# Due times of a list scheduler, nudged job by job from a table (linear attention and a token/channel mixer on one core)

## The chip, the core and the metric

The kernel runs on one core of one Trainium2 chip. The metric is the device time of one execution in microseconds (us); the runs shown are repeated executions of the same program. All times below are in microseconds unless marked ns.

## The reference

Inputs are q, k and v of 8 batches x 8 heads x 1024 positions x 64, two projections E and F (64 x 1024), and four mixer weights. Shortened:

```python
k_proj = einsum('ks,bhsd->bhkd', E, k)
v_proj = einsum('ks,bhsd->bhkd', F, v)
scores = q @ k_proj.T / sqrt(64)
attn   = softmax(scores)                       # over 64 projected positions
x      = attn @ v_proj                         # heads side by side: 8 x 1024 x 512
h      = maximum(x.T @ w_tok1, 0) @ w_tok2     # 1024 -> 256 -> 1024, over the positions
u      = x + h.T
out    = u + maximum(u @ w_ch1, 0) @ w_ch2     # 512 -> 1536 -> 512, over the channels
```

## The kernel before, in words

Each of the 8 batches goes through a front and a back. The front loads q, k and v (`load_heads`, L354, in halves of four heads from batch 1 on, on the POOL queue), projects k and v over the positions (`kv_proj`, matmuls at L492 and L495), brings kT and qT into place, computes scores (`scores`, L605, exponentials on ACT at L614), attends (`attend` or `attend_whole`, L628 and L664, division on DVE at L640, L645, L676 and L681), and runs the token mixer (`token1...`, `token2...`) to get u. From batch 2 on, kT and qT come from DMA transposes on SP's queue (L524 and L570), and u is turned to uT the same way in two halves (`turn_u`, L767). The back handles each batch in two blocks of 512 positions (16 blocks, counted by j): DVE forms sums S of quarters of uT (`s_sums`, L789), `up_set` forms seven products in place of eight for each of three slices of the channels (matmuls at L1152; ACT and DVE bring the results into G at L1174, L1180 and L1133, and DVE forms sums of G at L1188), and `down_block` multiplies G by the second weight, again with seven products (L1261), empties the banks on DVE (L1301, L1311) and stores (L1295, on the POOL queue; the last block's stores go on SP and ACT). Sums of the channel weights that the seven-product form needs are made on DVE at the start (`combine`, L452).

The order of all this is not written by hand. Every step is a `Job` with an engine, an estimated occupation and latency, dependencies, a claim on PSUM banks where it has one, and a due time `prio`. Due times are set by formulas: the back by `due_u` and `due_d` (24.65 units for each block), the front spread evenly between a beginning and an end by `front`, and steps without a due time get one from the steps that follow them. `Planner.plan` is a list scheduler: it walks through time, takes for each engine the jobs that can start within 0.02 of the earliest, and among these picks the one with the lowest due time. Its result is sorted by planned start and issued in that order. Each engine then works in that order, with semaphores for the dependencies; so the due times decide the order of the instructions on each engine, and nothing else. Three details matter below:

- Loads and stores to POOL's queue are marked `early`: they are put into the order at the time at which their dependencies end, not at which the planner lets them move. Loads that become free together keep the order in which the planner picked them.
- Loads and transposes take turns by added dependencies (`tie`). The first v half of a later batch has to have landed before the second half of u is turned; the second v half and q are issued after that transpose has landed; the two qT transposes wait for the last q load.
- The idle time of PE in the plan at the start is filled with matmuls on zeros (L413), as long as bank 5 is unused.

Before the scheduling loop, the due times of all jobs later than -30 get a pseudo-random offset of at most 0.8 either way, from the job's number and a seed.

Of the kernel before, what the change touches and what calls it, by code (L numbers as in the profile page):

```python
# [11 lines left out]
ALU = mybir.AluOpType  # L12
ACT = mybir.ActivationFunctionType
EARLY = 12.0
SHAKEN_FROM = -30.0
SHAKE = 1.6
SEED = 710
WHOLE = 3
TWO = 2
SUMS = 60.0  # L20
# [27 lines left out]
class Planner:  # L48
# [37 lines left out]
    def plan(self):  # L86
# [13 lines left out]
                j.prio = max((d.prio for d in j.deps), default=0) + 2  # L100


        for j in self.jobs:
            if j.prio > SHAKEN_FROM:
                j.prio += SHAKE * ((j.n * j.n * 7919 + j.n * SEED * 31 + SEED * SEED * 17) % 10007 / 10007 - 0.5)
        free = {}
        waiting = {j.n: len(j.deps) for j in self.jobs}
        can = {}
# [19 lines left out]
        def home(b, now):  # L128

            if held[b.stream] + b.span > self.caps[b.stream]:  # L130
                return None
            if b.span == 2:
                free2 = [
                    (max(now, bank_free[i], bank_free[i + 1]), i) for i in PAIRS[b.stream]
                    if bank_free[i] is not None and bank_free[i + 1] is not None
                ]
                return (*min(free2)[:1], 0, 0, min(free2)[1]) if free2 else None
            if b.stream in "UD" and turn[b.stream][0] is not b:
                return None
            best = None  # L140
            keep = [i for i in self.homes["U"] if clean[i] and bank_free[i] is not None]
            if all(clean[:5]):
                keep = []
            for i in self.homes[b.stream]:
                t = bank_free[i]
                if t is None or (b.seeded and not clean[i]):
                    continue
                if not b.seeded and clean[i] and keep and keep[-1] == keep[0] == i:
                    continue
                c = (max(now, t), clean[i], t, i)  # L150
                if best is None or c < best:
                    best = c
            return best

        while any(can.values()):
            pick = None
            for e, js in can.items():
                f = free.get(e, 0.0)
                cands = []
                for j in js:  # L160
                    t = max(f, est[j.n])
                    spot = None
                    if j.takes:
                        h = home(j.takes[0], t)
                        if h is None:
                            continue
                        t, spot = h[0], h[3]
# [4 lines left out]
                c = min((c for c in cands if c[0] <= t0), key=lambda c: (c[1], c[2]))  # L172
# [4 lines left out]
            t, _, _, j, spot = pick  # L177
# [4 lines left out]
            if j.takes:  # L182
                b = j.takes[0]
# [1351 lines left out]
```

## Time and profile before

| | us |
|---|---|
| median of 3 runs | 422.15 |
| lowest and highest run | 421.42, 422.19 |
| span of the profiled execution, first to last instruction | 420.3 |
| what lies around the span, against the median | 1.85 |
| PE busy | 410.3 |
| DVE busy | 347.5 |
| ACT busy | 231.3 |
| POOL busy | 66.2 |

The profile is of one execution, whose own time is given by its span alone; the granted TensorE clock was 1.000 over it. The five engines named are PE (matmuls; PEld is the loading of its weights), DVE, ACT, POOL and SP, which issues transposes and the last stores. A DMA's landing is told as the time from the start of its issue instruction. "Start to start" below is the distance of the starts of two matmuls that follow each other.

### The profile page before, as it was taken

The page shows a single profiled execution, that of the slowest core. Times are in us where ns is not written, and L with a number is a line of the kernel's source. Part 1 is how long each engine was busy: PE and PEld are TensorE (multiplying, and loading weights), DVE is VectorE, ACT ScalarE, POOL GpSimd, SP SyncE. Part 2 cuts the span into 40 slices and gives each one's busy share as a digit, 9 for nine tenths or more (in the row PEclk, how much of TensorE's full clock was granted, in tenths as well). Part 3 has the DMA queues.
Part 4 walks back from the last instruction along what each step waited for, and adds up shares of the span by engine and source line. Part 5 has one row for each costly group of instructions (what it writes and reads, how often), then busy time and mean ns, then how long its engine had stood idle before and what let it go on. Part 6 is the DMA issues. An engine that isn't in the chain of part 4 may idle for free.

```text
span 420.3 us, 9411 instructions
## 1 busy us (share of the span) xinstructions
PE 410.3 (98%) x3824; PEld 347.6 (83%) x3838; DVE 347.5 (83%) x747; ACT 231.3 (55%) x444; POOL 66.2 (16%) x104
## 2 busy tenths in 40 slices
PE   7899999999999999999999999999999999999996
PEld 4587877688788888888988898888798899988885
DVE  2359969679779798998979799797979999978685
ACT  2958885356646555555547455475655554454430
POOL 8443220022003030032002110112100000010010
PEclk9999999999999999999999999999999999999999
DMA  9999999989994989398998897395962501251223
GB/s 166 207 201 206 207 206 166 238 137 204 174 152 88 194 138 251 60 165 159 198 205 130 175 183 194 84 189 100 209 149 50 152 35 67 50 97 56 101 89 114
DMA packets 96668, 62.48 MB, mean 149 GB/s; under 512 B 62064, under 2 KB 92272, under 8 KB 96624
## 3 DMA queue, kind: packets, MB, share of 16 engines
q0 software_dynamic: 34944, 45.09, 54.9%
q1 hardware_dynamic: 61056, 16.00, 22.6%
q10 hardware_dynamic: 624, 0.79, 0.7%
q8 instruction: 30, 0.49, 0.4%
q14 instruction: 14, 0.11, 0.1%
HBM read 59.24 MB, written 16.78 MB: 181 GB/s over the span
## 4 chain that ended last, share of the span: by engine, by line
PE 87%; DMA 6%; DVE 4%; issue 1%; POOL 1%; ACT 0%; POOLq 0%; DVEq 0%
PE psum L1261 34%; PE psum L1152 33%; PE psum L856 4%; PE psum L972 4%; DMA v_sb<-in_v_dram 3%; DMA q_sb<-in_q_dram 3%; PE psum L492 3%; PE psum L605 3%; PE psum L664 2%; DVE u L1079 1%; PE psum L628 1%; PE psum L695 1%; PE psum L719 1%; PE psum L744 1%; PE psum L589 1%
## 5 line engine op out<-in xcount | busy, mean ns | idle before, releaser
L1261 PEld LDWEIGHTS <-G 128*128 128x128 bf16 x1344 | 130.4, 98 | 18.9 <-issue 0.6
L1261 PE MATMUL psum<-wc_sb,G 128*128 128x256 bf16 x768 | 102.9, 273 | 0.3 <-DVE wait L1301 0.3
L1174 ACT ACTIVATE G<-psum 128x512 bf16<-128x512 f32 x96 | 57.3, 599 | 56.8 <-PE psum L1152 56.5
L1152 PEld LDWEIGHTS <-wc_sb 128*128 128x128 bf16 x768 | 74.1, 98 | 10.2
L1261 PE MATMUL psum<-wT,G 128*128 128x256 bf16 x576 | 77.6, 273 | 0.3
L1188 DVE TENSOR_TENSOR G<-G 128x512 bf16<-128x512 bf16 (+1 forms) x140 | 69.6, 519 | 1.0
L1152 PEld LDWEIGHTS <-wT 128*128 128x128 bf16 x576 | 55.7, 98 | 9.0 <-issue 0.8
L1152 PE MATMUL psum<-S,wc_sb 128*128 128x256 bf16 x384 | 57.6, 273 | 0.2
L1152 PE MATMUL psum<-uT,wc_sb 128*128 128x256 bf16 x384 | 57.6, 273 | 0.0
L1152 PE MATMUL psum<-S,wT 128*128 128x256 bf16 x384 | 55.7, 273 | 0.2 <-DVE S L789 0.2
L1295 POOL DMA_DIRECT2D out_dram<-o x30 | 16.4, 546 | 240.3 <-DVE o L1301 160.5
L614 ACT ACTIVATE a<-psum 128x512 bf16<-128x512 f32 x64 | 36.7, 598 | 17.6 <-PE psum L605 16.5
L1301 DVE TENSOR_TENSOR o<-psum,u 128x512 f32<-128x512 f32 x55 | 37.6, 685 | 9.5 <-PE psum L1261 7.2
L1180 ACT COPY ua<-psum 128x512 f32<-128x512 f32 x48 | 28.2, 588 | 25.5 <-PE psum L1152 25.1
L1133 DVE CUSTOM_DVE_ANT_0 G<-psum,ub 128x512 bf16<-128x512 f32 x48 | 33.0, 687 | 9.1 <-PE psum L1152 8.9
L1133 DVE CUSTOM_DVE_ANT_0 G<-psum,ua 128x512 bf16<-128x512 f32 x48 | 33.0, 688 | 8.0 <-ACT ua L1180 7.8
L1195 ACT COPY psum<-psum 128x512 f32<-128x512 f32 x48 | 27.9, 580 | 14.5 <-PE psum L1152 5.3
L1180 ACT COPY ub<-psum 128x512 f32<-128x512 f32 x48 | 28.2, 587 | 9.4 <-PE psum L1152 8.3
L1152 PE MATMUL psum<-uT,wT 128*128 128x256 bf16 x192 | 28.8, 272 | 0.1
L681 DVE TENSOR_TENSOR x_sb<-psum,rdn 128x512 bf16<-128x512 f32 x40 | 27.5, 688 | 0.6
L605 PE MATMUL psum<-qT,kT 128*128 128x512 bf16 x54 | 19.8, 379 | 1.4 <-ACT kT L557 0.6
L354 POOL DMA_DIRECT2D v_sb<-in_v_dram x18 | 13.5, 751 | 45.8 <-DMA uT<-u 25.0
(108 smaller groups left out, 546.3 us busy)
## 6 DMA issues: line engine op xcount, KB each, us to landing
out_dram<-o POOLq DMA_DIRECT2D x30, 512.0 KB, 4.4
k_sb<-in_k_dram POOLq DMA_DIRECT2D x14, 512.0 KB, 9.5
v_sb<-in_v_dram POOLq DMA_DIRECT2D x14, 512.0 KB, 10.5
q_sb<-in_q_dram POOLq DMA_DIRECT2D x14, 512.0 KB, 9.4
wc_sb<-in_moe_w_ch_dram POOLq DMA_DIRECT2D x6, 256.0 KB, 12.4
wc_sb<-in_moe_w_ch_dram POOLq DMA_DIRECT2D x4, 384.0 KB, 12.2
k_sb<-in_k_dram POOLq DMA_DIRECT2D x4, 256.0 KB, 6.6
v_sb<-in_v_dram POOLq DMA_DIRECT2D x4, 256.0 KB, 7.2
```

The costliest lines, as they stand in the source:

```text
L605: lambda: nc.tensor.matmul(bank(bk), kT[:, h].rearrange("p c k -> p (c k)"), qT[:, h].rearrange("p j s -> p (j s)"), start=True, stop=True,),
L614: lambda: nc.scalar.activation(out=a_t[h // 2 % 2][:, h % 2], in_=bank(bk), func=ACT.Exp, scale=scale),
L681: lambda: nc.vector.tensor_tensor(out=x_sb[:, :, h * D : (h + 1) * D].rearrange("p (n c) d -> p n c d", n=2), in0=view()[:, :, :, 0:D], in ...
L856: nc.tensor.matmul(to, tok1_of(n, si), mv, start=(n == 1 and si == 0), stop=(si == NJ - 1), skip_group_check=True,)
L1133: nc.vector._custom_dve(TENSOR_ADD_SAT, out=out, in0=in0, in1=in1, s0=FMAX, s1=0.0)
L1152: nc.tensor.matmul(t[:, c, :], w1_of(n, dd, 2 * m + c), a_of(j, n, dd), start=(n in (1, 7) and c == 0 and dd == 0), stop=(c == 1 and dd == 1),
L1174: lambda: nc.scalar.activation(out=G[:, n, cs], in_=view(src), func=ACT.Relu),
L1180: 512, lambda: nc.scalar.copy(out=dst, in_=view("y")), writes=[(name, s % 2)],
L1188: 512 * len(both), lambda: f(out=G[:, n, c], in0=G[:, a, c], in1=G[:, b, c]), ps=False,
L1195: 512, lambda: nc.scalar.copy(out=view("y"), in_=view("x")), takes=[bk["y"]],
L1261: nc.tensor.matmul(to, G[:, G_OF[n], cc, t * P : (t + 1) * P], w2_of(n, cc), start=(n in opens and (t == 0 or alone) and cc == 0), stop=(c ...
L1301: 512, lambda: nc.vector.tensor_add(out=dst, in0=view(src), in1=u_of(sh, dh)),
```

## The change

The pseudo-random offset is replaced by one from a table: a string with one character for each job, in the order in which the jobs were added. A character's code less 80, times 0.25, is added to the due time; the characters in use reach from `$` to `}`, which is -11.0 to +11.25. The first 37 characters, and some others, are `P`, which is zero. The table was found by a local search on the planned program. Jobs, dependencies, durations in the planner, tiles and the functions that issue instructions are the same. The built program has 25 matmuls on zeros for 26; otherwise it has the same instructions in another order on every engine, and PSUM banks may be assigned otherwise.

```diff
-SHAKEN_FROM = -30.0
-SHAKE = 1.6
-SEED = 710
+STEP = 0.25
+MIDDLE = 80
+NUDGES = (
+    "PPPPPPPPPPPPPPPPPPPPPPPPPPPPPPPPPPPPPKa%Q]>f}YHB%VmgYjif?GOVZ}@}BpfO5CUF<`,o,TeHoVjRTChfR4S=;^NwbuhZ"
...
+    "v`}}}}rr}jrUY:]R?P/10("
+)
...
-        for j in self.jobs:
-            if j.prio > SHAKEN_FROM:
-                j.prio += SHAKE * ((j.n * j.n * 7919 + j.n * SEED * 31 + SEED * SEED * 17) % 10007 / 10007 - 0.5)
+        for j, c in zip(self.jobs, NUDGES):
+            j.prio += STEP * (ord(c) - MIDDLE)
```

What moves, as far as the two built orders show it: on POOL, stores and loads swap places from the third batch on, and loads of one group change their order; on SP, the place of kT among the two qT transposes in batches 2 to 5 and 7; on PE and DVE, the steps of the front against those of the back, by up to some ten microseconds of work, and the products of a block among each other. The last eight groups of matmuls of the last block (products 5, 2, 3 and 4) and the ten DVE steps that end the program keep their order.

More of the change, by code (lines that the diff above doesn't have):

```diff
@@ L14 @@
 EARLY = 12.0
-SHAKEN_FROM = -30.0
-SHAKE = 1.6
-SEED = 710
+STEP = 0.25
+MIDDLE = 80
+NUDGES = (
+    "PPPPPPPPPPPPPPPPPPPPPPPPPPPPPPPPPPPPPKa%Q]>f}YHB%VmgYjif?GOVZ}@}BpfO5CUF<`,o,TeHoVjRTChfR4S=;^NwbuhZ"
+    "IUGKS[W3H^98N7<TUMs8=OVUf][QuDVXxO]qwD8aR[XgOKSJTA8:Od6SMN'4DTiG.t0f]E]0bZf)f7gQDi_}Zo@FZE.Jm,V?6bT2"
+    "gZBOoPPPPPP+]EB:L?nhNP<RUS-J.MeIO*7$j5UI_L[8.BmbvePPN8BQqTbM[I)TlG:n2MK1[.)@BIh9G0,XtsmCHhvm,yb]<,d>"
+    "MR$FFC|ynr]AQ7EU5bfywyym`]G*N_*DM@AYcJDavgxmsmq]8aQ.06(*NEM]4AR`LtSn{f9,b$+$-.GUqE;E]Lcp[-@[Ykuz@V;O"
+    "HIRFWm^MO|kHV78-7fkm--Z/-<3F[D`}9<[UNGC:NHZaR3vjVXplnzswqbQMfDRlYI8fY|MT]8.<M:]:TbNUZd2]8O?PQ[kHCGRp"
+    "2P$>q,>G}fHlmmC-P]T3D8';{ROXa}V=}0TK@8=*6:82<n63@$773CS;+T[gOWJW,Ngkf$$$+&($(';Q4EPU0)f]0;2)%VMgH&2_"
+    "hEa`?A$/6$+PTUM04aDfHFr2[>,CCJ?^A&rtUl]WRhDR[m]g]MH{yd`?aQO9,0/-)$6=H`-%<%>F%%F0'R$[;w:h8Rfa0NL$canL"
+    "FC$G$${kb[[7fmlfkQ86NG8(}6_:R),165*576*]Gh2:Ml54Jh*&PZ8-rjeqgW1,$%:(&$'9RJ$RB,6LdBHYiT[dfZ]]]]-Wn=XU"
+    "]z$$:)]VBgdD+n^6_mvc}wwhsm}xw}v]OiZ{e`:;TL>YOa&f4>]mM[<cL]][aoRWDY$?YY}}}XR`FqL&&%60dLaXI+1rljVGI$J="
+    "Sv-5J[sD'8L5YZ{S<lf:2EEjrTE'(2D?<S9<.:/0XSO9A*-7$,1<6$.9+3^`?QFE7.MigwlZA;zaZ]NTQ@2&>FN$Z)*$,V1gU]`5"
+    "hA5Q?ANNkXUcjgWZab(EeU{|jbQLG[J_^g8@kP{ePE|]I6S&0Fiew[|m|vOB?Yo@N9EA`.]:2t.WWLH`kJfg{WQxg[R^SQwWnO}E"
+    "fD93=J?J_Q^UYbEGTQ|g`h]?&JHgb`gSI)9rQUfkSdCADY0c$2yQ2./ZI;M]4K.GBE9*H.31^gaNdodFc,-AY:oYfThnn{adLK;4"
+    "S(4/cpb|DmO2V{RlLMST;O*E4,'_5hA)C:85.FZ]s9ROI2Lib($/,'U'66eF<T*9I;D/($'&'4-Y)=(c]A`X=Zc92.3DD1h-&[nw"
+    "]Wvz{frUrhrfF'9%ibB+$J$$V>JE1aJutZh1me00kDjt}R}>i5KJ}Q^iu]}}mF>;}N}{vw[R{^w:Px4]6&WT]CQ>38(OvN{u+xUS"
+    "USr}Ol:>s}NI[R4P`Ae:@]3WMFQY^g`NfYhyv|}2;;&IciBM_)jhp;VqrF]scw}}}t}[qK>LdC}}}FSU2P'ZAEBF78oLkRLdKL.C"
+    "jDOZkLvyKI1QTGDB2(%>HL^we'YIr<7B7OuKetXgWHsXmvU`VnTUwss>|rB]oC*OV-/OIKr$BDRMJb@}anh9YO*b=g}YMh1h}aD^"
+    ".fG}}pWt},<^^jc:7K=<:z)-4$(($-PNP9MT=*7$Q7_aOm|bk0}f$}OtBMG/}rN]GiHIk=e4qk22WebZ3F-jW@M.Ph&>`OuzE$b]"
+    "}|`i{}I`_9iMhXSj99M><3XQk+$XD>+*h&I2f]n8qL/4*a3]q}IRBI-87]4j_s]N:Pep3A?63<UX40QY1>8,Q:J(o*(9(*&lV7^b"
+    "oRROGqFfozup[X52f}(duwq]|w{lifTfNlAlZH$km$JbmQB1F$S_[0{jT_KXC=6DcrGN:.>SS:QDB$4R*E?OlZsmffFaCc$gZF7t"
+    "XYaTew@`fYNXd$cx]eIqO/@)J0,)3,N'?4O,9),:=ca7-/2ZOJ;G$3-I%S%K%$F[4YD0(A]0I'9xoSc]LOCO:'-4-V-?CXgTgC9K"
+    "B^^rgk3R-$1/$5EAFF^Y$&t-b9?$=.F`]cg|WE8al}h>}^]tsgrv]@EMGBcVZVgT@NhGsX[]dY]rN]gdu|[w}>t]>T[O]]$>*5]P"
+    "GRI1{70dO]`rusrNEdVub$_C2L-::d{jbcGY=+oMJJh5)[LtM<O(tm^P`>WKM1+Al-]N]_I>iJMR_G6C&@ZI`GTXlWP3C2]QSIDi"
+    "v`}}}}rr}jrUY:]R?P/10("
+)
```

## The prediction

> **What bounds it now.** I read the page's busy line first, then the stretches of the span, the waits of PE, the chain that ended last around 31 us, the SP queue around 73 us and single places of the timeline. All times are microseconds.
>
> ```profile
> PE 410.3 (98%) x3824; PEld 347.6 (83%) x3838; DVE 347.5 (83%) x747; ACT 231.3 (55%) x444; POOL 66.2 (16%) x104
> ```
>
> PE is the bound, and this change issues the same matmuls. The second view, busy time by stretch (length, then PE, PEld, DVE, ACT, POOL, clock, DMA share, GB/s), says where PE is not busy:
>
> ```profile
> 0.00:40.00 40.00, 35.18 (x387) 25.27 (x391) 21.58 (x66) 24.94 (x57) 22.96 (x38) 1.00 1.18 194
> 40.00:100.00 60.00, 59.39 (x551) 47.45 (x553) 50.55 (x137) 38.97 (x74) 8.36 (x12) 1.00 1.09 194
> 100.00:120.00 20.00, 19.63 (x169) 15.98 (x168) 15.66 (x33) 11.45 (x23) 2.81 (x4) 1.00 1.06 173
> 120.00:408.00 288.00, 287.63 (x2650) 251.76 (x2656) 252.77 (x501) 155.35 (x291) 31.79 (x50) 1.00 0.67 132
> 408.00:416.60 8.60, 8.48 (x77) 7.11 (x74) 6.52 (x14) 0.57 (x1) 0.26 (x1) 1.00 0.30 113
> ```
>
> Half of the 10.0 idle is the start (4.82, most of it inputs coming in at 166 to 207 GB/s), 3.70 lies behind the last matmul. Between 40 and 416.6 only 0.61+0.37+0.37+0.12 = 1.47 is shown. That understates a wait: a 256-column matmul is drawn 273 ns long, while eight of them in the chain take 0.87, so they follow each other every 0.109, and up to 0.164 of each wait lies under the drawn tail of the matmul before. What an order can win is thus small: a handful of waits of 0.15 to 0.6. The waits of PE name them:
>
> ```profile
> PE psum L1093 <- DVE u L1079: 0.6, 2, 0.4
> PE psum L1261 <- DVE wait L1301: 0.3, 1, 0.3
> PE psum L495 <- DMA v_sb<-in_v_dram: 0.3, 1, 0.3
> ```
>
> **What the new order removes.** Only the instruction order of the two built programs is used, with durations from the trace. One filler matmul on zeros goes (25 for 26); it filled a wait, so it counts nothing.
>
> (a) Start, 30 to 36. The chain runs through DVE, and in it stand the channel-weight sums between the additions that PE waits for:
>
> ```profile
> 31.88 0.33 DVE wc_sb L452
> 33.41 0.33 DVE wT L452
> 34.94 0.33 DVE wT L452
> ```
>
> Between the second addition to u and the first S sum the old DVE order has four such sums, the new one two: 2 x 0.33 = 0.66 off that chain. PE waits 0.44+0.20 at L1093 and 0.17 at the S sum, 0.8 in all. The moved sums still have to be there for the first products from wT, so I take 0.5 (0 to 0.8).
>
> (b) At 88. PE waits 0.34 as drawn, and from start to start 0.5, for the DVE addition that empties the bank of product 3 of a down block:
>
> ```profile
> 88.55 0.81 PE L1261 MATMUL psum<-wc_sb,G 128*128 128x256 bf16 x6 [0.34 <-DVE wait L1301]
> ```
>
> Between product 5 and product 3 of that block PE has two attends and one scores now, 2 x 0.113 + 0.216 = 0.44; in the new order an up product of four matmuls stands there too, 0.88. The added 0.44 covers nearly all: 0.4 (0 to 0.5).
>
> (c) At 109, the v load for batch 3. It was issued at 102.71 behind a store of 101.64, landed 7.29 later, and PE lost 0.5. Its issue waits for the second transpose of u (96.32 to 102.14), which waits for the first v half, second of three loads then (landed 96.26). The new POOL order puts that v half first: issued 87.35, it lands after the 5.43 that the first of the three took, at 92.8; transpose 5.82, issue 0.57 later, load 5.4: 104.6. The new PE order reaches this projection 37 matmuls (4.1) earlier, at 109.3-4.1 = 105.2 before the other terms, which move it by about 0.1. It is just in time: saves 0.5 (0 to 0.5).
>
> (d) End. After the last sums of G PE's weight load waits 0.40, from start to start 0.3:
>
> ```profile
> 409.00 7.32 PEld L1261 LDWEIGHTS <-G 128*128 128x128 bf16 x68 [0.40 <-DVE G L1188]
> ```
>
> Twelve matmuls (1.31) now stand between the last up product 4 and product 7, whose sums need 2.0 (406.97 to 409.00). In the new order 34 matmuls (3.7) stand there. Saves 0.3 (0 to 0.4).
>
> (e) Four small waits (39.9, 60.6, 162.2, 260.0; 0.28, 0.15, 0.16, 0.13 from start to start) may go or be replaced by others: I take half, 0.4 (-0.3 to 0.7).
>
> Sum: 0.5+0.4+0.5+0.3+0.4 = 2.1.
>
> **What it adds.** (f) SP's queue, batch 2. Today it runs, with a scores matmul as first reader (start, time in the queue):
>
> ```profile
> 72.80 4.11 SPq L570 DMA_TRANSPOSE qT<-q_sb  x1
> 77.01 2.27 SPq L524 DMA_TRANSPOSE kT<-kb  x1
> 79.33 2.45 SPq L570 DMA_TRANSPOSE qT<-q_sb  x1
> 84.22 0.38 PE L605 MATMUL psum<-qT,kT 128*128 128x512 bf16 x1
> ```
>
> They land 7.94, 4.50 and 5.77 after issue: at 80.75, 81.52 and 85.10. The first scores need kT and the first qT half (81.52, 2.7 spare); the second half is read from 91.7. The new SP order is second half, first half, kT. Both halves are still held until the last q load lands (72.66; those loads keep their POOL order), so the sequence starts at 72.8 again, and now the first scores need all three. In PE's new queue they stand at the same place (779 matmuls ahead, 780 before), so at 84.2 less (a): 83.7. Bounds: kT issued third, at 79.3, and landed after the shortest kT time of the trace, 3.0, is there at 82.4 and costs nothing; landing when the third does now, 85.1, costs 1.4. The 16 engines are full over 72.8 to 85.1 (DMA share 1.01) and the same bytes move, so I stand near the later end: 1.0 (0 to 1.5). Behind the waiting scores stand all PE work, then ACT's exponentials, then DVE's divisions; nothing is hidden.
>
> [...]
>
> (g) The rest of POOL and SP: stores and loads swap places, and kT goes last in batches 3 and 7 too, to the middle in 4 and 5. The tightest of these is batch 3: its first scores stand at about 120.9 (105.2 plus 15.7 of PE work in between); with the v load landed at 104.6 its q loads land 2.5 and 5.1 after it (110.00, 112.54 and 115.13 now), the transposes start at 107.1 and, at batch 2's 12.3 for all three, end at 119.4: 1.5 spare. Taken at nothing (-0.2 to 1.0).
>
> Net: 2.1 - 1.0 = 1.1 off the profiled 420.3, so 419.2. The page's span lies 1.85 under the median of 422.15; nothing in the change touches what lies around the span, so 421.05: **421.0**. About 0.2% (0.84) is what a measurement of this kernel can tell from no change, so faster means under 421.3.
>
> **Rivals.** *Transposes in time.* kT passes quickly or PE arrives later; (f) costs nothing. For it: kT's 3.0 to 3.4 on a quiet queue. Against: the queue isn't quiet there. 422.15-2.1 = 420.05, 0.23.
>
> *Slower: the v load of batch 5.* Its projection moves up by 93 matmuls, 10.2, from 211.14 to 200.9, less 0.4 net gained by then: 200.5. Before, its load was third of three, issued 197.80, landed 11.0 later. Now it is first; the transpose of u that releases it stands 3.05 earlier in PE's work, so lands at 192.8 for 195.81, and the load is issued at 193.3. At 5.4 it lands at 198.7, 1.8 spare. At 10.9, the median of the loads issued third behind two others, it lands at 204.2 and PE stands 3.7: 421.05+3.7 = 424.8. It makes the kernel slower once the load takes over 9.2 (stall over 1.94). Against: it is issued first, and loads issued first took 5.3 to 5.6 in six places. 0.15.
>
> *Nothing to see.* The waits taken away come back a few instructions later, since DVE stays 83% busy: 422.1, within 0.8 either way, 0.20.
>
> The forecast gets 0.42, its own range 420.3 to 421.8.
>
> **Numbers.** Faster: 0.27 of the forecast's 0.42, all 0.23 of the first rival, 0.04 of the last = 0.54. Same: 0.15+0.12 = 0.27. Slower: 0.15+0.04 = 0.19. The range runs from 419.6 (first rival with larger savings) to 423.2, which leaves out the worse half of the v load's 0.15 and as much again at the two ends of the others.
>
> **What would show it.** Right: SP's order qT, qT, kT with kT landing near 85 and a PE idle of about 1 at L605 near 84; no idle at the L1261 by 88, none at L495 for v_sb near 105; the L1093 waits under 0.3; PE idle by 408 gone. Wrong: a wait on v_sb at 200, a kT landing by 83, or new DVE waits of PE in 120 to 400 that sum to over 1.

## The result, and the profile after

The changed kernel takes 425.98 us (median of 11 runs, 424.69 to 433.06), the kernel before 422.38 beside it (11 runs, 421.42 to 424.66): ratio 1.009, 95% interval 1.0066 to 1.0114. It is 3.6 us slower; 1.1 us faster was forecast. The run of 433.06 counts as slow and is left out of the ratio. The profiled execution is a long one, 430.54 with a span of 428.8; the first experiment gives the profile of an ordinary one.

In the changed kernel's lines everything behind the table stands 23 lines further down than before: L354 is now L377, L495 is L518, L605 is L628, L1152 is L1175, L1261 is L1284. First its busy line and the row of granted clock in 40 slices:

```profile
PE 412.9 (96%) x3826; PEld 349.3 (81%) x3837; DVE 348.4 (81%) x747; ACT 232.4 (54%) x444; POOL 66.2 (15%) x104
PEclk8999999998999999999999999999989999999999
```

The span has grown by 8.5, PE's busy time by only 2.6; that part is mostly matmuls at a lower clock, as the slices below show. Busy time by stretch (length, PE, PEld, DVE, ACT, POOL, clock, DMA share, GB/s) says where:

```profile
100.00:120.00 20.00, 17.22 (x140) 13.50 (x139) 13.08 (x30) 10.32 (x21) 2.76 (x4) 0.91 1.02 175
120.00:300.00 180.00, 179.83 (x1659) 155.94 (x1660) 159.99 (x318) 99.65 (x185) 25.69 (x38) 1.00 0.83 152
300.00:320.00 20.00, 16.51 (x134) 13.00 (x132) 12.97 (x28) 10.37 (x21) 1.10 (x2) 0.91 1.01 189
```

Two stretches of 20 hold nearly all of it; the 180 between them are as full as before. PE's waits name three tiles, all brought by DMA, where before the DMA waits behind the start were the 0.3 for v_sb alone:

```profile
PE psum L518 <- DMA v_sb<-in_v_dram: 3.5, 1, 3.5
PE psum L1175 <- DMA uT<-u: 2.7, 1, 2.7
PE psum L628 <- DMA kT<-kb: 0.8, 1, 0.8
```

On PE's timeline they stand in this order:

```profile
84.59 0.82 PE L628 MATMUL psum<-qT,kT 128*128 128x512 bf16 x3 [0.82 <-DMA kT<-kb]
103.55 0.82 PE L1175 MATMUL psum<-uT,wc_sb 128*128 128x256 bf16 x3 [2.72 <-DMA uT<-u]
310.29 0.38 PE L518 MATMUL psum<-v_sb,FT_sb 128*64 128x512 bf16 x1 [3.49 <-DMA v_sb<-in_v_dram]
```

From start to start they are 0.98, 2.89 and 3.68, 7.55 in all. The queue of SP for the first two:

```profile
72.68 8.44 SPq L593 DMA_TRANSPOSE qT<-q_sb  x2
81.22 1.25 SPq L547 DMA_TRANSPOSE kT<-kb  x1
...
93.02 5.94 SPq L790 DMA_TRANSPOSE uT<-u  x1
```

kT is issued third and lands at 84.54. The second half of uT is issued at 93.02, 3.30 earlier than before, and lands at 103.50: 10.48 after its issue, where it took 5.82 before. Before, its transpose and the first product that read it stood at

```profile
96.32 3.76 SPq L767 DMA_TRANSPOSE uT<-u  x1
103.55 0.60 PE L1152 MATMUL psum<-uT,wc_sb 128*128 128x256 bf16 x4
```

and PE did not wait. In the changed kernel POOL's queue has brought in, beside the transpose,

```profile
88.18 0.77 POOL L377 DMA_DIRECT2D k_sb<-in_k_dram  x1
89.27 0.75 POOL L377 DMA_DIRECT2D k_sb<-in_k_dram  x1 [0.33 <-issue]
93.79 0.55 POOL L1318 DMA_DIRECT2D out_dram<-o  x1 [3.77 <-DVE rdn L663]
```

two k loads, landing at 96.87 and 100.29, and has sent out a store, landing at 102.27. The load that held PE at 306.4 is the v half of batch 7, issued third in its group at 298.25, behind both q loads; it lands 11.99 later. Before, it was the first of the three, issued at 290.92 and landed 5.52 later, and PE did not wait.

The waits are not the whole of it. The stretch around the second wait in slices of 1 us (the clock is the third number from the end):

```profile
102.00:103.00 1.00, 0.00 (x0) 0.00 (x0) 0.00 (x0) 0.00 (x0) 0.00 (x0) 1.00 1.01 225
103.00:104.00 1.00, 0.45 (x3) 0.33 (x4) 0.48 (x2) 0.00 (x0) 0.00 (x0) 0.63 0.00 0
104.00:105.00 1.00, 1.00 (x8) 0.84 (x7) 1.00 (x3) 0.33 (x1) 0.97 (x2) 0.50 0.00 0
...
106.00:107.00 1.00, 1.00 (x8) 0.75 (x7) 1.00 (x3) 0.49 (x1) 0.80 (x2) 0.66 0.65 88
107.00:108.00 1.00, 1.00 (x11) 0.89 (x10) 1.00 (x3) 0.55 (x2) 0.00 (x0) 1.00 1.23 206
```

PE works again from 103.55, but at half clock until about 106.7: some 3 us at half speed, 1.5 lost. Behind the wait at 306 the clock falls too, but later, when PE has been at work again since 310.29:

```profile
311.00:312.00 1.00, 1.00 (x10) 0.53 (x7) 0.00 (x0) 0.00 (x0) 0.00 (x0) 0.74 1.17 174
312.00:313.00 1.00, 1.00 (x5) 0.28 (x3) 0.00 (x0) 0.24 (x1) 0.00 (x0) 0.50 1.26 369
```

It is at 1.00 again from 315.

### The profile page after: what moved, and what is told of

It is laid out like the page before. It is cut to its first block, busy times and chain, and to the rows that moved or that the text cites. A ratio compares the mean times of both kernels' runs of the same rounds, so it can differ in the third digit from the quotient of the medians.

```text
span 428.8 us, 9422 instructions
## 1 busy us (share of the span) xinstructions
PE 412.9 (96%) x3826; PEld 349.3 (81%) x3837; DVE 348.4 (81%) x747; ACT 232.4 (54%) x444; POOL 66.2 (15%) x104
## 4 chain that ended last, share of the span: by engine, by line
PE 84%; DMA 7%; issue 3%; ACT 2%; DVE 2%; POOL 0%; POOLq 0%
PE psum L1284 32%; PE psum L1175 31%; PE psum L879 4%; PE psum L995 4%; PE psum L515 3%; DMA v_sb<-in_v_dram 3%; PE psum L628 3%; DMA uT<-u 2%; PE psum L687 2%; DMA o<-in_F_dram 1%; PE psum L1090 1%; PE psum L718 1%; PE psum L651 1%; PE psum L612 1%; DMA kT<-kb 1%
## 5 line engine op out<-in xcount | busy, mean ns | idle before, releaser
L1284 PEld LDWEIGHTS <-G 128*128 128x128 bf16 x1344 | 130.8, 98 | 18.7 <-issue 0.2
L1284 PE MATMUL psum<-wc_sb,G 128*128 128x256 bf16 x768 | 103.3, 273 | 0.0
L1175 PEld LDWEIGHTS <-wc_sb 128*128 128x128 bf16 x768 | 74.5, 99 | 13.6 <-DMA uT<-u 3.0
L1284 PE MATMUL psum<-wT,G 128*128 128x256 bf16 x576 | 76.1, 273 | 0.1
L1175 PEld LDWEIGHTS <-wT 128*128 128x128 bf16 x576 | 55.8, 98 | 8.5 <-issue 0.2
L1175 PE MATMUL psum<-uT,wc_sb 128*128 128x256 bf16 x384 | 58.2, 276 | 2.9 <-DMA uT<-u 2.7
L1175 PE MATMUL psum<-S,wc_sb 128*128 128x256 bf16 x384 | 57.5, 273 | 0.0
L1175 PE MATMUL psum<-S,wT 128*128 128x256 bf16 x384 | 56.5, 274 | 0.2
L1175 PE MATMUL psum<-uT,wT 128*128 128x256 bf16 x192 | 28.8, 273 | 0.1
L377 POOL DMA_DIRECT2D v_sb<-in_v_dram x18 | 13.5, 749 | 69.0 <-DMA uT<-u 44.6
L628 PE MATMUL psum<-qT,kT 128*128 128x512 bf16 x57 | 20.8, 379 | 2.0 <-DMA kT<-kb 0.8
```

Of the source, the lines that this page charges most:

```text
L628: lambda: nc.tensor.matmul(bank(bk), kT[:, h].rearrange("p c k -> p (c k)"), qT[:, h].rearrange("p j s -> p (j s)"), start=True, stop=True,),
L1175: nc.tensor.matmul(t[:, c, :], w1_of(n, dd, 2 * m + c), a_of(j, n, dd), start=(n in (1, 7) and c == 0 and dd == 0), stop=(c == 1 and dd == 1),
L1284: nc.tensor.matmul(to, G[:, G_OF[n], cc, t * P : (t + 1) * P], w2_of(n, cc), start=(n in opens and (t == 0 or alone) and cc == 0), stop=(c ...
```

## The experiments

The edits move jobs in the planned order and nothing else; how they do so is shown in full once, and the comments in the code are added here. All were timed beside the kernel before, whose median was 422.85 (e1 to e4), 422.87 (e5 to e8), 422.58 (e9 to e12) and 422.70 (e13 to e15).

**The changed kernel again (e1), and v ahead in batches 6 and 7 (e2).** e1 has no edit. e2:

```diff
-        return sorted(order, key=lambda j: j.at)
+        out = sorted(order, key=lambda j: j.at)
+        by = self.jobs
+        out.remove(by[1708])                                # second v half, batch 7
+        out.insert(out.index(by[1956]) + 0, by[1708])       # ahead of its q loads
+        out.remove(by[1448])                                # batch 6
+        out.insert(out.index(by[1696]) + 0, by[1448])
+        return out
```

> The changed kernel once more, to see which of its waits recur. Theory (three waits on DMAs make the loss: kT at 84, the second half of uT at 101, the last v load at 306, and a slow clock after the long ones): wait for kT 0.8 to 1.0; for uT about 2.9 with the clock near 0.54 for some 3.5 us behind it; the wait for v at 306 differs between executions, 0 to 3.7; time about 426.0. Rival (the slow clock comes by itself and the order only makes small waits everywhere): slow stretches at other places, and a drift against the plan of before between the three places.

> Only the order on POOL's queue of the loads that are freed together for batches 6 and 7: v ahead of the two q loads. Theory: the v load lands 5.5 after issue instead of 12, no wait of PE for v near 302 to 306, clock 1.00 from 300 to 320; where the execution had that wait it is 5.5 shorter (3.7 wait and 1.8 slow clock); median 425.0 to 425.7. Rival (the DMA queues are full there, so the wait moves to the q transposes): a wait of 2 or more at the scores of batch 7 and the time unchanged.

e1: 425.09 (424.60 to 427.66), ratio 1.0065 [1.0045, 1.0086]. Its profiled execution, 424.92, is an ordinary one. Its waits of PE for transfers, behind the start:

```profile
PE psum L1175 <- DMA uT<-u: 2.1, 1, 2.1
PE psum L518 <- DMA v_sb<-in_v_dram: 0.9, 1, 0.9
PE psum L628 <- DMA kT<-kb: 0.9, 1, 0.9
```

The v wait here is that of batch 3, at 108 (1.12 from start to start). For the v half of batch 7 PE does not wait: it lands at 306.06, just as PE comes to it. With kT's 1.05 and uT's 2.27 the waits make 4.4, and the clock stays up, as this slice just behind the uT wait shows (14 matmuls in 1 us, where the other execution did 8):

```profile
104.00:105.00 1.00, 1.00 (x14) 0.91 (x11) 1.00 (x5) 0.81 (x2) 1.00 (x2) 1.00 0.00 0
```

e2: 425.31 (424.46 to 426.68), 1.0062 [1.0045, 1.0079], level with e1. The v half now lands at 302.87 and PE doesn't wait for it, but in the ordinary execution there was little to win there. So batch 7 can explain the long executions, not the ordinary loss; that one lies at 84 to 110. In e2's profile kT cost 2.06 (landed 85.87), and behind its wait for uT, 2.30 as drawn, the clock is at 0.50 (behind e1's, 2.11, it is at 1.00):

```profile
104.45 0.96 PE L1181 MATMUL psum<-uT,wc_sb 128*128 128x256 bf16 x4 [2.30 <-DMA uT<-u]
105.00:106.00 1.00, 1.00 (x8) 0.88 (x7) 0.99 (x5) 0.50 (x1) 1.00 (x2) 0.50 0.00 0
```

**kT between the two qT transposes in batch 2 (e3); a store moved behind the loads of batch 3 (e4).** In place of e2's moves:

```diff
+        out.remove(by[650])                                 # e3: first qT transpose
+        out.insert(out.index(by[656]) + 1, by[650])         #     behind kT
...
+        out.remove(by[368])                                 # e4: first store of block 2
+        out.insert(out.index(by[372]) + 1, by[368])         #     behind v, q, q of batch 3
```

> Only SP's order in batch 2: first q half, kT, second q half, as before the change. Theory (from 87 on the DMA chain uT first half, v, uT second half sets the time, whatever PE does before): the wait for kT at 84 goes (0.8 to 1.0), the wait for uT at 101 grows by as much; time unchanged within 0.3, 426.0. Rival (the waits add up independently): 0.8 to 1.0 shorter, 425.1.

> Only one store (512 KB, issued at 93.8 beside the second transpose of u) moved behind the v and q loads that follow that transpose. Theory (loads, store and transpose share full DMA engines): the transpose lands about 2.4 earlier, near 101, wait at the product 0.5 for 2.9, no slow clock behind it; the v load for batch 3 lands near 107 and its projection waits about 1.3; together some 2.4 shorter, 423.6. Rival (the transpose is slow by itself right behind the v load): it lands at 103 as before and the time stays 426.

e3 is a miss in an instructive way: 427.07 (425.80 to 429.89), 1.0112 [1.0083, 1.0142]. The wait for kT is gone, and PE pays for it at once:

```profile
PE psum L1179 <- DMA uT<-u: 4.1, 1, 4.1
```

uT lands at 104.17 (103.41 in e1, 104.40 in e2), when it lands anyway; PE only gets there earlier. Two short waits have become one long one, and behind that the clock is 0.50 up to about 109.7. With the first of two waits in a row taken away, the median stands 2.0 above e1's. With six runs each, and the v load of batch 7 still third, that size is rough; that nothing was gained is clear.

e4: 426.01 (422.45 to 429.36), 1.0067 [1.0036, 1.0097], but its twelve runs fall into two groups, six from 422.45 to 424.87 and six from 427.15 up. The profiled execution is of the first group, 423.01. uT takes 8.07 in place of e1's 9.96 and lands 2.3 sooner:

```profile
PE psum L522 <- DMA v_sb<-in_v_dram: 0.9, 2, 0.7
PE psum L632 <- DMA kT<-kb: 0.7, 1, 0.7
PE psum L1179 <- DMA uT<-u: 0.2, 1, 0.2
```

**Both (e5), two stores and kT (e8).** e5 is e2 and e4 together. e8 has e2's and e3's moves, and the last store of block 1 and the first of block 2 behind the loads:

```diff
+        out.remove(by[368])
+        out.insert(out.index(by[915]) + 1, by[368])         # 915: last q load of batch 3
+        out.remove(by[291])
+        out.insert(out.index(by[915]) + 1, by[291])
```

> The changed kernel with two moves on POOL's queue together: the store of e4_store_later goes behind the second v half and the two q loads of batch 3, and in batches 6 and 7 the v half goes ahead of the two q loads with which it becomes free, as in e2_v_first. Theory: the loss sits in two transfers, the second half of uT near 101 and the v load of batch 7 near 304, each slowed by transfers that were put beside or ahead of it; and in e4_store_later the upper group of times (427.2 to 429.4) came from the batch-7 v load being third. Then the waits at 99 to 109 sum to about 1.3 as in that run (0.4 and 0.9), there is none on v_sb near 303, the time is 422.4 to 423.4, within 0.5 of the kernel before, and no run stands above 425. Rival: the upper group belongs to the uT transpose, which lands late in some executions; then the times spread up to 427 or more here as well, and the median stays near 426.

> The changed kernel with v ahead in batches 6 and 7, kT second in batch 2, and two stores (the second of block 1 and the first of block 2, 512 KB each) moved from ahead of and beside the loads of batch 3 to behind its v and q loads. Theory: over 72 to 110 the DMA engines are full, so what helps the uT and v waits is fewer bytes there; a store of this size shifted the chain by 2 to 3 (e4_store_later: uT landed 2.3 sooner, v 2.7), so two shift it by 4 to 6, kT lands by 82, uT by 99, the v half by 104.5, and no wait over 0.5 is left between 80 and 110: the savings of the new order show, 419.9 to 421.3, under the kernel before by 1 to 2.5. Rival: the deferred stores collide with the transposes for batch 3 at 110 to 121 and a new wait of 1 to 3 stands at the scores near 120: 421.5 to 424.

e5: 422.77 (422.45 to 423.91), 0.9994 [0.9976, 1.0012]. The upper group is gone, so it came from the v load of batch 7 (no run of that group was profiled); with it and the store out of the way the change costs nothing. e8: 421.73 (420.87 to 423.15), 0.997 [0.9953, 0.9987], faster than both kernels.

**Compute order and transfer order apart (e6, e7).** The planned order is walked through by its compute jobs, and the transfers are put between them as the other kernel's queues have them, as soon as their dependencies are met:

```diff
+DMA_ORDER = (0, 1, 2, ...)     # e6: of the kernel before; e7: the changed kernel's
...
+        for j in out:
+            if j.eng not in ("DMA", "POOL"):
...
+                put(j)         # and behind it what of POOL's and SP's queues is free
```

> PE, DVE and ACT in the changed kernel's order; POOL's and SP's queues in the order of the kernel before. Theory: the compute order itself asks for the second half of uT and for the second v half of batch 3 earlier than the full DMA engines can bring them, in whatever order: uT landed at 102.14 and v at 110.00 in the kernel before, PE now comes to them at about 99.5 and, with the first wait, 107; so about 2.5 and 3 are waited there, no kT wait near 84 and none for v in batch 7: 424 to 427, as slow as the changed kernel or nearly. Rival: the new order of the loads, stores and transposes is what costs, and the compute order is good: then no wait over 0.6 stands at 99 to 110 and the time is 420 to 421.5.

> PE, DVE and ACT in the order of the kernel before; POOL's and SP's queues in the changed kernel's order. Theory: at 84 PE waits 1.0 for kT, third in its group; at 99 to 110 nothing or under 0.5, because PE comes 3 to 4 later to uT and v than in the changed kernel; for the v half of batch 7, third in its trio, PE waits about 4.5, since it comes to it at about 298 to 299 and the third of three loads takes 10.4 to 12.0 from its issue near 291; with the slower clock behind such a wait 427 to 429. Rival (the new DMA order costs at 100 too): 2 to 4 of waits at 99 to 110 as in the changed kernel, 429 to 432.

e6: 442.06 (440.60 to 443.68), 1.045 [1.0416, 1.0485]. The sign is that of the theory, the size isn't: I had counted only the waits at 100 and 107. PE's long idle times stand in three batches:

```profile
105.39 1.04 PE L1210 MATMUL psum<-uT,wc_sb 128*128 128x256 bf16 x4 [5.00 <-DMA uT<-u]
161.77 1.01 PE L1210 MATMUL psum<-uT,wc_sb 128*128 128x256 bf16 x4 [4.53 <-DVE G L1191]
220.62 0.64 PE L553 MATMUL psum<-v_sb,FT_sb 128*64 128x512 bf16 x1 [6.45 <-DMA v_sb<-in_v_dram]
```

The second is behind a half of uT as well, for which PE's weight load waited:

```profile
160.71 0.10 PEld L1210 LDWEIGHTS <-wc_sb 128*128 128x128 bf16 x1 [3.75 <-DMA uT<-u]
```

That transpose was issued at 156.41, when the v half ahead of it, third of its group, had landed (156.27). The third is the v half of batch 5, third of its group in the old order (issued 210.51, landed 220.57). The changed kernel puts both v halves first, and needs to. From start to start the three waits make 16.5, and half speed behind them costs 6.5 more.

e7: 425.90 (425.16 to 430.89), 1.0085 [1.005, 1.0121], 2 to 3 less than expected. Nothing is waited for at 99 to 110, although uT takes 9.76 here: the old compute order comes 3 later. In its profile kT costs 0.83, a DVE result at 240 1.53, and v of batch 7 only 1.01, since it landed 9.78 after its issue. So each order is bad with the other's transfers. The loss at 100 comes only with the new compute order, which reads uT and v sooner; e4 shows that with one store out of the way most of the wait for uT goes even so.

**How long a wait has to be (e11, e12), in the kernel before.** The second v half of batch 3 goes behind both q loads, or behind one:

```diff
+        out.remove(by[660])
+        out.insert(out.index(by[916]) + 1, by[660])         # e11; e12: by[915]
```

> The kernel before with one exchange on POOL's queue: the second v half of batch 3 is issued behind the two q loads with which it becomes free, in place of ahead of them. The landings of this group in the kernel before were 110.0, 112.5 and 115.1, and PE stands at the projection at 109.5. Theory (a long wait costs more than itself, because the granted clock falls to 0.5 some 2.5 after PE stops and stays there for some 3.5 after it starts again, which is 1.7 more): wait of 5.3 in place of 0.5 and 1.7 of slow clock: 422.5 + 4.8 + 1.7 = 429, 428 to 430. Rival (the wait alone counts, the slow stretch is made up for later by engines that have run ahead): 426.5 to 427.5.

> As e11_before_v_third, with the v half second, between the two q loads. It lands at about 112.5; PE waits 2.9. The waits of 2.3 in e1_again and 2.7 in the changed kernel stand on either side of the point at which the clock fell. Theory: a wait of 2.9 is past it, so 422.5 + 2.4 + 1.7 = 426.6, 425.8 to 427.3, with matmuls at half speed for about 3.5 behind the wait. Rival: the clock falls only after more than 3 without work: then 424.9, 424.4 to 425.4, and a granted clock of 1.0 behind the wait.

e11: 429.83 (429.37 to 430.35), 1.0174 [1.0153, 1.0195]; e12: 427.23 (426.17 to 428.81), 1.0114 [1.0089, 1.0138]. The two idle times, e11's first:

```profile
115.43 0.58 PE L499 MATMUL psum<-v_sb,FT_sb 128*64 128x512 bf16 x1 [5.54 <-DMA v_sb<-in_v_dram]
```

```profile
113.93 0.59 PE L499 MATMUL psum<-v_sb,FT_sb 128*64 128x512 bf16 x1 [3.40 <-DMA v_sb<-in_v_dram]
```

From start to start 5.72 and 3.59, against the 0.51 that the kernel before waits there: 5.2 and 3.1 more. The medians rose by 7.25 and 4.65. The difference, 2.0 and 1.6, is half speed for 4.3 (115.4 to 119.8) and 3.1 (113.9 to 117.0). Nothing of a wait was made up for later. e12's idle time came out at 3.40, longer than the 2.9 that was meant to test the rival's bound of 3; e2's 2.30, with the clock at 0.50 behind it, is what speaks against that bound.

**The savings by hand (e9), and the worth of the compute order (e10, e13, e14, e15).** e9 and e15 start from the kernel before, e10 and e14 add one exchange to e8, e13 is e8 again:

```diff
+        out.remove(by[38])                                  # e9: sums of L452,
+        out.insert(out.index(by[211]) + 0, by[38])          #     38, 39 and 40 go
...                                                          #     among the first S sums
+        out.remove(by[291])                                 # e9 and e15: 291, 368, 372
+        out.insert(out.index(by[916]) + 1, by[291])         #     behind the loads
...
+        out.remove(by[917])                                 # e10, e14: e8, and the first qT
+        out.insert(out.index(by[924]) + 1, by[917])         #     half of batch 3 behind its kT
```

> The kernel before with two small parts of the change made by hand and nothing else: three of the four channel-weight sums (L452) that stand between the additions to u move behind the first S sums, and three stores (the second of block 1 and both of block 2) go behind the v and q loads of batch 3. Theory: each takes away one wait of PE that the trace shows: about 0.5 at 33 to 36 and the 0.5 for the v half at 109, which now lands by 106, since its group is issued without 1.5 MB ahead of it; nothing else moves: 421.4 to 422.0, 0.2 to 0.3% under the kernel before, and equal within 0.5 to e8_two_stores_later, so that the table of the change brings nothing that these moves do not. Rival: the new compute order keeps its own savings (at 88, at the end, small waits: 1.1), so this version stays 0.7 to 1.5 above e8_two_stores_later's 421.7.

> e8_two_stores_later with one more exchange on SP's queue: in batch 3 too kT goes between the two qT transposes in place of behind both. Theory: the wait of 1.1 at the scores near 122 was for a kT issued third (119.05, landed 123.51); issued second at 115.5 it lands by 121 and the wait goes, or half of it where the second qT half takes its place: 0.5 to 1.1 less than e8_two_stores_later, 420.6 to 421.3, no wait over 0.3 near 122; the 1.0 for v at 105 stays. Rival: the first scores also need bytes that the three deferred stores hold up, so PE waits there as long for another tile: 421.5 to 422.0.

> e8_two_stores_later once more, beside the next two on one chip. What is open is whether the compute order of the change keeps a gain once the transfers are out of PE's way: e8_two_stores_later stood 1.1 under the kernel before, e10_kt_second_twice, with one wait less in its profile, level with it. Theory (the compute order is worth the 2.1 that the prediction summed; kT costs nothing here, and the waits left for v near 105 and kT near 122 cost 1.0 and 1.1 less the 0.5 that the kernel before waits for v): 0.4 to 1.2 under the kernel before. Rival (the order gains nothing that lasts; the 1.1 was scatter between runs): within 0.3 of the kernel before.

> e10_kt_second_twice once more, beside e13 and e15. Theory: one wait of 1.1 less than e13_two_stores_again, so 0.5 to 1.1 under it and 1.0 to 2.0 under the kernel before. Rival: level with the kernel before as in its first run, and not under e13_two_stores_again, so that a wait at 122 that goes is met again before the end.

> The kernel before with only the three stores moved behind the v and q loads of batch 3, as in e9_before_two_parts, and the channel-weight sums left where they were. Theory: the wait of 0.5 for v at 109 goes and nothing else changes: 0.3 to 0.6 under the kernel before; what e9_before_two_parts gained there, its moved sums lost at 33 to 36 (1.6 of waits there against 1.3). Rival: the v wait is met again by the next one, so the time stays within 0.2 of the kernel before, as in e9_before_two_parts.

e9: 422.49, 1.0001 [0.999, 1.0011]; e15: 422.14, 0.9993 [0.9973, 1.0013]. Neither can be told from the kernel before. In both the 0.5 for v at 109 is gone; in e9 the waits at 33 to 36 grew from 1.30 to 1.60, so my copy of the first step was a bad one.

e13: 421.54, 0.9972 [0.996, 0.9984], as e8 was. e10: 422.63, 0.9997 [0.9981, 1.0013]; e14: 422.88, 0.9998 [0.9984, 1.0013]. The expectation that one exchange more would win 0.5 to 1.1 failed twice: e10 stood 0.9 above e8, e14 1.3 above e13. e13 still waits for the batch-3 v half, and not near 122; e14, where kT comes second, does:

```profile
105.80 0.38 PE L530 MATMUL psum<-v_sb,FT_sb 128*64 128x512 bf16 x1 [0.71 <-DMA v_sb<-in_v_dram]
```

```profile
122.67 0.38 PE L642 MATMUL psum<-qT,kT 128*128 128x512 bf16 x1 [1.16 <-DMA qT<-q_sb]
```

The wait near 122 moved from kT (1.09 in e8's profile) to the qT half issued third (1.32 from start to start, landed 122.53). In the kernel's code job 917, which the edit puts behind kT, is the transpose of heads 0 to 3, and the first scores read it. So the edit is not e3's: e3 leaves the first half first. It brought kT forward by putting back another transfer that the same scores need. e13's and e10's profiled executions have no wait there. With one profile for each run, how often it occurs in each order stays open.

e13 against e15 gives an estimate of the worth of the compute order, the stores being out of the way in both: 0.6 in the medians, and e13 still waits 1.27 at 99 to 105 (0.37 for uT, 0.90 for v), e15 nothing. So the order itself wins about 1.9. That goes by one profile each, and the runs behind the 0.6 overlap (420.96 to 422.47 and 421.44 to 425.24).

## Why the prediction was wrong

**The savings were there.** In the changed kernel's profiles, the first and e1's, the waits at 33 to 36 fell from 1.30 to 0.97 (a: 0.3, predicted 0.5), the 0.50 at 88 is gone (b: predicted 0.4), the 0.28 at the end is gone (d: predicted 0.3). Of the four small waits of (e), 0.72 in all, e1's profile has none and has two others of 0.18 and 0.13 (0.4, as predicted). That makes 1.5 where 1.6 was predicted without step (c); the estimate from e13 and e15 is 1.9. The two DVE sums and the weight load that stood in the prediction now read

```profile
34.45 0.42 DVE L475 TENSOR_TENSOR wc_sb<-wc_sb 128x512 bf16<-128x512 bf16 x1
...
411.93 2.61 PEld L1284 LDWEIGHTS <-G 128*128 128x128 bf16 x24
```

two sums are left ahead of the first S sum at 34.78 (at 30.48 and the one shown) in place of four, and the weights of G carry no idle bracket.

**(f) held:** kT third, landed 84.54 and 85.07, cost 0.98 and 1.05 where 1.0 was said; of the six profiles with kT third, five have 0.83 to 1.11 and e2's has 2.06. In all 17 profiles no transpose on SP's queue landed before one issued ahead of it; the closest two landed 0.77 apart in the kernel before (80.75 and 81.52) and 1.12 apart in the first profile of the changed one (316.34 and 317.46). But the 1.4 that the prediction gives for kT landing at 85.1 was too much for that profile: issued last, kT took only 3.3 (81.22 to 84.54).

**(c) failed, and made the sign.** It said: v half first, so uT is issued earlier, takes 5.82 again, and the next v load lands at 104.6. The first half came true (v landed 92.96 against 92.8, uT issued 93.02). The step that failed is the transpose's 5.82: it took 10.48, and 9.96 in e1. Issued earlier, it lay beside two k loads (landed 96.87 and 100.29) where it had lain beside one (landed 98.94), and its time was not its own:

| kernel | group of loads starts | uT issued | took | landed | landing less start | stores issued from 90 to 100 |
|---|---|---|---|---|---|---|
| e15 | 86.61 | 94.50 | 5.30 | 99.80 | 13.2 | 0 |
| e4 | 87.57 | 93.00 | 8.07 | 101.07 | 13.5 | 0 |
| before | 87.35 | 96.32 | 5.82 | 102.14 | 14.8 | 1 |
| after | 87.43 | 93.02 | 10.48 | 103.50 | 16.1 | 1 |
| e6 | 88.06 | 96.76 | 8.58 | 105.34 | 17.3 | 2 |

Over all 17 profiles, three loads and one transpose take 13.2 to 14.0 whichever load comes first if no store is issued from 90 to 100 (eight profiles). With one store they take 14.8 to 15.0 in the old order of the loads (three) and 15.2 to 16.1 with v first (five); with two, 17.3 (e6). So what v won by going first the transpose lost. The row behind 5.82 was one in which two of the three loads had landed when uT was issued. Since the 16 engines are full over this stretch (DMA share 0.98 from 87.35 to 102.14 before; I had used that for kT and not here), the term should have been priced by bytes. An estimate that leaves both landings where the kernel before has them gives uT near 102 and v near 110, so that PE, moved up by 4.1, waits. I priced the load behind the transpose and did not look at who else reads uT: its first product stood at 103.55 and moved to 100.66. That is 2.3 to 2.9 lost where 0.5 was to be won; 1.1 more for v where the clock stays up, 1.5 for the clock where it falls. For e1 the sum then comes out: 1.5 saved, less 1.05 for kT, 2.27 for uT and 0.6 more for v than before, is 2.4 lost, and 2.2 was measured.

**(g) was taken at nothing for the wrong reason.** I searched it for its tightest place and named the scores of batch 3. The v half of batch 7 had gone from first to third in its group, a move that I had listed only as loads changing their order. In the five profiles that have it third it landed 9.8 to 12.0 after issue (9.78, 10.07, 10.26, 10.35, 11.99), in those that have it first 5.3 to 5.5. The changed kernel waited 3.68 for it in the first profile and not at all in e1; e4's profile, of its lower group, has 0.43. That a wait like the 3.68, with the slow clock behind it, makes the upper group of e4 is what its absence in e5 says; no profile shows it.

**The rival on the other side had the right mechanism and the wrong batch.** It charged 3.7 for a v load that lands as a third one does, in batch 5. There the load was first, took 5.53 as "against" said, landed at 199.02, and nothing waited. In batch 7 the same price was paid in the first profile (3.68).

**The term that no case held is the clock.** A long idle time was charged at its own length; e11 and e12 show 1.6 to 2.0 on top.

All that was listed to show it right came in the changed kernel's first profile, and nothing of what was to show it wrong: no wait for v_sb at 200, kT not by 83, no new DVE waits. (In e1's the v half of batch 3 was waited for near 108.) The list watched the places that I had already thought of; a list that could have caught this one has the sum of PE's waits for DMA in it.

What the local search saw in this order can be read in its plan. There, this half of uT lands 5.5 after its issue in either order; in the new order it is planned from 89.9 to 95.4, and its first reader at 97.4 in place of 101.0. The plan became 2.5 shorter (418.6 for 421.1), part of it by asking earlier for a transfer that doesn't come earlier.

## What to carry to other kernels

Where the DMA engines are full, price a transfer by the bytes that have to pass before it, and not by the duration that its row shows: here reordering within a full stretch (DMA share 0.98 over the kernel before's 87.35 to 102.14, 1.02 over the changed kernel's 87.43 to 103.50) did not bring the last landing forward (13.2 to 14.0 in either order, and 14.8 to 16.1 with one store among them), so an order that brought its reader forward turned into a wait. For each load whose rank in its group changes, and each transfer, look for its first reader in the new order, in every batch. A search over a planned program can lean on places where the plan is too kind, as it did here; a few moves of stores, loads and one transpose by hand turned a loss of 2.2 to 3.6 (e1 and the first result) into a gain of 1.1 to 1.2 (e8, e13).

## What the runs showed of the hardware

Behind the longer idle times of PE the granted clock was 0.50, and such a wait cost more than itself: 1.6 more in e12, 2.0 in e11. Idle times of PE as drawn, and the clock behind them: 1.90 (e2) and 2.11 (e1), 1.00 all through; 2.30 (e2), 0.50 from just about the restart; 2.72 and 3.49 (after), 3.40 (e12), 4.12 (e3), 4.53, 5.00 and 6.45 (e6) and 5.54 (e11), 0.50. Worked out from slices of 1 us, it fell 2.4 to 5.1 after the end of the last matmul as drawn, twice when PE was already at work again (e2, and after at 311.5). It came back 2.9 to 5.5 after the first matmul, which costs 1.4 to 2.8. The nine stretches at half clock behind these idle times lasted, by the same slices, either 3.4 (five of them: after twice, e2, e12 and one of e6's) or 6.8 (four: e3, e11 and two of e6's).

The DMA transpose of one half of u took 5.30 from its issue to its landing in e15 and 10.48 in the changed kernel's first profile, in the same place of the program, and the profiles differ in what POOL's queue brought in ahead of it and beside it (the table above).
